# Attention and two dense layers on one core: rounded q and k made and moved two slots sooner, a bank of its own for head 0's unread products, residues of heads 1 and 2 on GpSimd

## The chip, the cores and the metric

The kernel runs on 1 core of a Trainium2 chip. The metric is the device time of one execution in microseconds (us). TensorE does the matmuls, VectorE (DVE in the rows), ScalarE (ACT) and GpSimd (POOL) the elementwise work, SyncE (SP) issues nearly all transfers. A matmul of TensorE writes to PSUM, in eight banks; the other data are in SBUF. Each engine takes its own instructions in the order in which they are written; between engines there are semaphores, placed by the framework where two instructions touch the same data.

## The reference

Attention for 2 batches, 8 heads, 768 positions and a head size of 64, with a mask by hash buckets; then two dense layers (512 to 2048 to 512) over 1536 tokens. Cut to what matters here:

```
q_bits = (einsum('bhsd,dk->bhsk', q, proj) > 0)      # 6 bits a position
k_bits = (einsum('bhsd,dk->bhsk', k, proj) > 0)
mask   = bucket(q_bits)[:, :, :, None] == bucket(k_bits)[:, :, None, :]
scores = where(mask, q @ k.T / sqrt(D), -1e9)
attn   = exp(scores - max(scores)); attn /= sum(attn) + 1e-9
x      = attn @ v                                    # then the dense layers
x      = (g(x @ w_in)) @ w_out                       # g = h * tanh(softplus(h))
x      = (P(x @ w_in2) / Q(x @ w_in2)) @ w_out2
```

## The kernel before, in words

**Numbers in two parts.** Matmuls run on float32 numbers that are rounded for TensorE (fp32r). A value is therefore kept as a rounded part ("hi") and a residue ("lo" = value - rounded part). For a head h, raws[h] holds k on partitions 0 to 63 and q on partitions 64 to 127. From it the kernel makes:

- qB[h % 4], by hi(h) on ScalarE (line 229, helper line 61): the rounded k and q. Later its rows 0 to 31 are overwritten with the signs of the codes, by code_q(h), two ScalarE activations (line 329).
- qX[h % 4], by lo(h) (line 234): the residue. The helper is lo_dve on VectorE (line 70) or lo_pool on GpSimd (line 67); the table ENG names VectorE for "lo".
- KK[h % 4], two planes of k: move_k(h) (line 241) is a DMA that copies the rounded k, qB rows 0 to 63, into rows 64 to 127 of both planes (384 KB in the DMA's count). For head 0 two ScalarE activations, khi, do that (line 237). move_x(h) (line 247) copies the residue of k into the second plane, move_h(h) (line 251) copies rounded q to the lower half of qX. code_k(h) (line 320, two VectorE instructions) writes the code rows of the first plane.

**The codes.** codes(h) (line 298) multiplies raws[h] with the projection into a PSUM tile "cp", of the tag "dn", which has one bank. code_k(h) reads the k half of it, code_q(h) the q half. For head 0 the product is made twice, and code_q reads the second copy, in the tile "wm" of the tag "pv" (one bank too). That tile is also the one that warm(n) writes: small matmuls whose results nobody reads (line 314), issued to keep TensorE at work in the start.

**The loop over keys.** For each head and each of 6 chunks of 128 keys: smax(h, c) (line 343) multiplies for the largest score, and VectorE reduces it (line 347); fin_a and fin_b (lines 353 to 365) turn the maxima into a row of qB[h % 4], by two DMAs on SP's queue and two on GpSimd's; st(h, c) (line 376) makes the scores, ScalarE the exponential (line 381); pv(h, c) (line 393, helper line 287) multiplies with v; dsum(h, c) (line 402) sums the exponentials into the tile "dn", of the same single bank as the codes. At the head's end evac and devac (lines 418 and 427) copy the results out of PSUM on ScalarE, gather(h) (line 436) brings the sums together by two small DMAs, recip(h) (lines 448 to 454) inverts them on VectorE.

**The order.** All of that is written out by hand in slots, six to a head. The table `order` (line 535) gives each step the slot, relative to the head's first st, in which its first piece is issued; within a slot the steps go in the order of the table's lines. Slots modulo 6 are called slot 0 to 5 here. In the steady state:

- slot 0: hi's new place; slot 1: fin_a, fin_b, evac, devac, move_h, and move_k's new place
- slot 2: hi's old place, codes, code_k, gather; slot 3: move_k's old place, lo
- slot 4: code_q, recip; slot 5: dsum (two pieces of the three), move_x, load

Heads 0 to 2 and head 1's first chunks are issued ahead of slot 0, in the order of the tuple `start` (line 599). There, an entry with a name in the set DVE_LO gets lo_dve as its helper, which the table ENG would give it as well.

Beside the heads, `weights` converts the first dense layer's weights (int64 words that hold float64 numbers), one part of a tile every six slots: load, three VectorE instructions (lines 100 to 106), two on GpSimd (lines 64 and 67), stores to a scratch for the first three tiles. The dense layers (lines 628 to 851) come after the heads.

Of the kernel before, what the change touches and what calls it, by code (L numbers as in the profile page):

```python
# [9 lines left out]
F32 = mybir.dt.float32  # L10
# [12 lines left out]
HALF = S // 2  # L23
# [4 lines left out]
NBITS = 6  # L28
EARLY, SHARED, FIRST = 7, 3, (78, 66, 72, 60, 60, 60, 60)
W_AT, W_LEAD = 7, 4  # L30
DVE_LO = (("lo", 0),)
ENG = dict(
    lo="dd", hi="aa", xhi="a", xlo="dd", whi="pppp", wlo="pppp",
)
# [10 lines left out]
def attention_moe_moe(ctx: ExitStack, tc: tile.TileContext, kq, v, proj2, cst, eye, w1, w2, ab, out):  # L45
    nc = tc.nc

    def pool(stack, name, bufs=1, **kw):
        return stack.enter_context(tc.tile_pool(name=name, bufs=bufs, **kw))
# [120 lines left out]
    def attention(actx, tctx):  # L170
# [10 lines left out]
        ps = pool(actx, "ps", 3, space=PSUM)  # L181
        pvp = pool(actx, "pv", 1, space=PSUM)
# [11 lines left out]
        ones = v_p.tile([128, 32], F32, tag="ones", name="ones")  # L194
        wones = v_p.tile([128, 128], F32, tag="wones", name="wones")

        def memsets():
            nc.vector.memset(ones, 1.0)
            nc.vector.memset(wones, 1.0)
            nc.gpsimd.memset(cs_t, 0.0)  # L200
            nc.gpsimd.memset(cs_t[:, 1:2], -1.0)
            nc.gpsimd.memset(cs_t[:, 2:3], 1.0)
            for i in range(4):
                nc.gpsimd.memset(f32(KK[i])[32:64, 0], 0.0)
            for i in range(2):
                nc.gpsimd.memset(f32(SM[i]), 0.0)
            nc.gpsimd.memset(bias[:, 1:2], 1.000001)
# [77 lines left out]
        def both(o, w, x, start=False, stop=False):  # L285
            for a in range(2):
                nc.tensor.matmul(out=o[64 * a:64 * a + 64, 0:HALF], lhsT=w, rhs=qhalf(x, a), start=start, stop=stop)  # L287
# [7 lines left out]
        ct = {}  # L295


        def codes(h):
            if not 0 <= h < B * H:
                return  # L300
            ct[h] = [pvp.tile([128, 512], F32, tag="dn", name="cp")] * 2
            if h == 0:
                ct[h][1] = warm_up[0]
            for t in ct[h][0:1 + (h == 0)]:
                both(t, p_raw, raws[h], start=True, stop=True)


        warm_up = []

        def warm(n):  # L310
            if not warm_up:
                warm_up.append(pvp.tile([128, 512], F32, tag="pv", name="wm"))
            for _ in range(n):
                nc.tensor.matmul(out=warm_up[0][0:32, HALF:512], lhsT=ones, rhs=wones, start=True, stop=True)  # L314

        def code_k(h):
            if not 0 <= h < B * H:
# [202 lines left out]
        def first(f, n):  # L520
# [16 lines left out]
            ("smax", smax, -11, 6),  # L537
            ("fin_a", fin_a, -5, 1),
            ("fin_b", fin_b, -5, 1),
            ("hi", hi, -16, 1),  # L540
            ("move_k", move_k, -15, 1),
            ("lo", lo, -15, 1),
            ("codes", codes, -16, 1),
            ("pv", pv, (3, 3, 5, 5, 7, 7), 6),
            ("dsum", dsum, (5, 5, 5, 5, 7, 7), 6),
# [41 lines left out]
        def slot_ops(g):  # L587
            for name, fn, k in slots.get(g, ()):
                if (name, k) not in done:
                    fn(*k)  # L590
# [5 lines left out]
        def coef():  # L596
            nc.scalar.activation(out=babs, in_=ab_t[:, 4:6], func=ACT.Abs)

        start = (
            ("load", 0), ("get", 0), ("get", 1), ("load", 1), ("load", 2), ("warm", 5), ("hi", 0), ("codes", 0),  # L600
            ("khi", 0, 0), ("lo", 0), ("warm", 5), ("code_k", 0), ("code_q", 0), ("hi", 1), ("khi", 0, 1), ("get", 2),
            ("move_k", 1), ("lo", 1), ("move_x", 0), ("smax", 0, 0), ("warm", 2), ("smax", 0, 1), ("warm", 2), ("hi", 2),
            ("smax", 0, 2), ("warm", 2), ("move_k", 2), ("lo", 2), ("move_h", 0), ("smax", 0, 3), ("warm", 2),
            ("smax", 0, 4), ("warm", 2), ("smax", 0, 5), ("codes", 1), ("fin_a", 0), ("fin_b", 0), ("code_q", 1),
            ("code_k", 1), ("load_v", 0), ("move_x", 1), ("load", 3), ("warm", 8), ("smax", 1, 0), ("smax", 1, 1),
            ("move_h", 1), ("coef",),
        )

        def run():
            memsets()  # L610
            fns = {o[0]: o[1] for o in order}
            fns.update(get=get, coef=coef, khi=khi)
            for name, *k in start:
                if name == "warm":
                    warm(*k)
                    continue
                done.add(("move_k" if name == "khi" else name, tuple(k[:1]) if name == "khi" else tuple(k)))
                fns[name](*k, **({"fn": lo_dve} if (name, *k) in DVE_LO else {}))
            for g in range(last):
                slot_ops(g)  # L620

        def tail(i):
            for g in {1: range(last, last + 3), 2: range(last + 3, last + 5), 4: range(last + 5, last + 30)}.get(i, ()):
                slot_ops(g)

        return run, tail

    def moe(mctx, tctx, tail):
# [224 lines left out]
    with tc.manual_schedule():  # L853
        nc.scalar.preload_act_table_set("natural_log_exp_and_others")
        tctx = ExitStack()
        with ExitStack() as actx:
            run, tail = attention(actx, tctx)
            run()
        with ExitStack() as mctx:
            run = moe(mctx, tctx, tail)  # L860
            run()
# [55 lines left out]
```

## Time and profile before

| what | value |
|---|---|
| median of 3 runs | 820.53 us |
| the three runs | 820.53, 812.40, 820.99 us |
| the profiled execution | 819.36 us, of which its span, first to last instruction, is 817.6 us |
| TensorE busy | 784.3 us (96%) |
| VectorE, ScalarE, GpSimd busy | 593.8, 424.9, 65.4 us |
| first st matmul of head 0 | at 21.95 us |
| first matmul of the dense layers | at 287.43 us |

Times in rows are us from the span's start unless marked ns. Groups of instructions are told by line of the kernel, engine, operation, and output<-input by the program's names. "[2.60 <-ACT qB L329]" behind a row says that the engine was idle for 2.60 us before it and that ScalarE's instruction of line 329 ended that idle time. Such releasers are inferred from semaphore events. A busy TensorE is not one at full speed: PEclk is the mean granted clock as a share of the full one, and of the two levels, 2.4 and 1.2 GHz, the lower reads 0.5. At the start of a span, before the first change of level, the record shows 1.00 whatever the level was.

### The profile page before, as it was taken

The numbers are of one execution on the slowest core, as the hardware profiler recorded it, in microseconds if no ns is written. First come the engines' busy times: TensorE is split into PE (matmuls) and PEld (weight loads), VectorE is DVE, ScalarE is ACT, GpSimd is POOL, SyncE is SP. The second block draws the span as 40 slices with busy tenths as digits, with TensorE's granted clock in tenths as the row PEclk, the third lists the DMA queues.
The fourth block names the chain that finished last, engine by engine and source line by source line (L and its number), as shares of the span: only waits on it lengthen the run. The fifth ranks groups of instructions, "written<-read, shape, count | busy, mean of one in ns | idle before, by whom it ended". The sixth has DMA issues, their size and how long they took to land.

```text
span 817.6 us, 10933 instructions
## 1 busy us (share of the span) xinstructions
PE 784.3 (96%) x3804; PEld 577.2 (71%) x3804; DVE 593.8 (73%) x1102; ACT 424.9 (52%) x684; POOL 65.4 (8%) x98
## 2 busy tenths in 40 slices
PE   8888989899989999999999999999999999999998
PEld 4444545455545577888888888887788888888886
DVE  5565677678775269965555667739999888888886
ACT  3344555456545544432122224448887766777674
POOL 2212132222221100000000000000000000000000
PEclk9899999999999999999999999999999999999999
DMA  4735455554564044442545467750000100001001
GB/s 117 201 103 156 130 139 149 152 143 121 146 176 138 22 127 128 144 141 81 176 156 153 149 202 248 233 162 26 0 1 1 52 1 1 1 1 52 1 0 52
DMA packets 57030, 85.49 MB, mean 105 GB/s; under 512 B 20496, under 2 KB 28688, under 8 KB 56976
## 3 DMA queue, kind: packets, MB, share of 16 engines
q1 hardware_dynamic: 55952, 84.77, 35.5%
q8 instruction: 30, 0.49, 0.3%
q14 instruction: 24, 0.20, 0.1%
q0 software_dynamic: 1024, 0.03, 0.1%
HBM read 57.71 MB, written 14.73 MB: 89 GB/s over the span
## 4 chain that ended last, share of the span: by engine, by line
PE 84%; DMA 6%; DVE 4%; ACT 3%; issue 1%; SPq 1%; POOL 0%; ACTq 0%; DVEq 0%
PE h L661 29%; PE y L681 16%; PE y L679 14%; PE sp L376 8%; DMA kk<-qB 6%; PE pv L287 5%; PE dn L402 5%; PE mp L343 4%; PE cp L287 2%; ACT qB L329 2%; PE wm L314 1%; DVE t L103 1%; DVE w L70 1%; DVE r L106 1%; DVE t L100 0%
## 5 line engine op out<-in xcount | busy, mean ns | idle before, releaser
L661 PE MATMUL h<-xh,w 128*128 128x512 f32 x768 | 205.0, 389 | 0.0
L661 PEld LDWEIGHTS h<-xh,w 128*128 128x128 f32 x768 | 144.1, 188 | 30.6 <-issue 0.6
L347 DVE TENSOR_REDUCE m<-mp 128x1 f32<-128x768 f32 x96 | 90.9, 954 | 73.3 <-PE mp L343 72.7
L381 ACT ACTIVATE e<-sp 128x768 f32<-128x768 f32 x96 | 77.2, 811 | 73.6 <-PE sp L376 73.2
L70 DVE TENSOR_TENSOR gl<-ep,gh 128x512 fp32r<-128x512 f32 x96 | 65.9, 686 | 61.5 <-ACT ep L705 60.8
L704 ACT ACTIVATE gh<-h 128x512 fp32r<-128x512 f32 x48 | 28.7, 598 | 154.6 <-PE h L661 141.5
L661 PE MATMUL h<-xl,w 128*128 128x512 f32 x384 | 102.7, 389 | 0.0
L681 PE MATMUL y<-w,gh 128*128 128x512 f32 x384 | 96.3, 389 | 0.0
L679 PE MATMUL y<-gh,w 128*128 128x512 f32 x384 | 94.8, 389 | 0.0
L661 PEld LDWEIGHTS h<-xl,w 128*128 128x128 f32 x384 | 72.1, 188 | 15.0
L679 PEld LDWEIGHTS y<-gh,w 128*128 128x128 f32 x384 | 72.1, 188 | 15.0
L681 PEld LDWEIGHTS y<-w,gh 128*128 128x128 f32 x384 | 72.1, 188 | 14.9
L287 PE MATMUL pv<-e,vf 128*64 128x384 f32 x384 | 72.5, 499 | 0.0
L402 PE MATMUL dn<-e,ones 128*32 128x384 f32 x384 | 42.2, 547 | 22.0 <-ACT qB L329 22.0
L376 PE MATMUL sp<-qB,kk 128*128 128x384 f32 x192 | 56.7, 376 | 1.6 <-DMA qB<-stt 1.1
L376 PEld LDWEIGHTS sp<-qB,kk 128*128 128x128 f32 x192 | 31.7, 194 | 37.2 <-issue 19.1
L711 ACT ACTIVATE ep<-h 128x512 f32<-128x512 f32 x48 | 28.5, 594 | 52.4 <-PE h L661 52.4
L106 DVE SCALAR_TENSOR_TENSOR r<-r,t 128x256 int32<-128x256 int32 (+1 forms) x114 | 52.2, 458 | 4.7
L343 PE MATMUL mp<-kk,qB 128*128 128x384 f32 x192 | 53.3, 360 | 2.1 <-issue 1.5
L103 DVE SCALAR_TENSOR_TENSOR t<-r,t 128x256 int32<-128x256 int32 (+1 forms) x114 | 52.2, 458 | 3.9
L681 PE MATMUL y<-w,gl 128*128 128x512 f32 x192 | 53.3, 392 | 0.5 <-DVE gl L70 0.4
L679 PE MATMUL y<-gl,w 128*128 128x512 f32 x192 | 51.6, 390 | 1.6 <-DVE gl L70 1.6
(78 smaller groups left out, 1010.2 us busy)
## 6 DMA issues: line engine op xcount, KB each, us to landing
r<-w SPq DMA_DIRECT2D x100, 256.0 KB
w<-r SPq DMA_DIRECT2D x64, 128.0 KB
w<-w SPq DMA_DIRECT2D x16, 512.0 KB
r<-w SPq DMA_DIRECT2D x14, 512.0 KB
kq<-kq SPq DMA_DIRECT2D x16, 384.0 KB
kk<-qB SPq DMA_DIRECT2D x15, 384.0 KB
kk<-qX SPq DMA_DIRECT2D x16, 192.0 KB
qX<-qB SPq DMA_DIRECT2D x16, 192.0 KB
```

The source lines that it names most:

```text
L70: nc.vector.tensor_tensor(out=o, in0=i, in1=f32(h), op=ALU.subtract)
L103: lambda: nc.vector.scalar_tensor_tensor(out=t, in0=r[:, :, 1], scalar=-0x40000000, in1=t, op0=ALU.bitwise_and, op1=ALU.bitwise_or),
L106: lambda: nc.vector.scalar_tensor_tensor(out=o, in0=r[:, :, 0], scalar=29, in1=t, op0=ALU.logical_shift_right, op1=ALU.bitwise_or),
L287: nc.tensor.matmul(out=o[64 * a:64 * a + 64, 0:HALF], lhsT=w, rhs=qhalf(x, a), start=start, stop=stop)
L343: nc.tensor.matmul(out=p[:, a, 0:HALF], lhsT=qB[h % 4][:, c * 128:(c + 1) * 128], rhs=qhalf(KK[h % 4][:, 0], a), start=True, stop=True,)
L347: nc.vector.tensor_reduce(out=mt[h][:, c:c + 1], in_=halves(p), op=ALU.max, axis=AX.XY)
L376: nc.tensor.matmul(out=p[:, a, 0:HALF], lhsT=kk[:, c * 128:(c + 1) * 128], rhs=qq[:, a * HALF:(a + 1) * HALF], start=(i == 0), stop=(i == 1),)
L381: nc.scalar.activation(out=wide(e), in_=halves(p), func=ACT.Exp, scale=1.0 / D ** 0.5)
L402: nc.tensor.matmul(out=pvt[h, "d"][32 * n:32 * n + 32, 0:HALF], lhsT=ones, rhs=qhalf(pt[h, c - 1 + n // 2], n % 2), start=(c == 1), stop=( ...
L661: nc.tensor.matmul(out=p, lhsT=w[:, c * 128:(c + 1) * 128], rhs=x[:, c, :], start=(n == 0), stop=(n == 11))
L679: nc.tensor.matmul(out=y[m], lhsT=w[:, DM + m * 128:DM + (m + 1) * 128], rhs=g, **s)
L681: nc.tensor.matmul(out=y[m], lhsT=g[:, m * 128:(m + 1) * 128], rhs=w[:, DM:2 * DM], **s)
```

## The change

- In the steady order, hi moves from slot -16 to -18 and move_k from -15 to -17, both relative to the head's first st. This holds for heads 3 to 15.
- In the start, lo of heads 1 and 2 gets lo_pool, GpSimd's helper; DVE_LO goes.
- warm writes to a tile of the pool "s" until the codes of head 0 are issued; the second copy of head 0's product has a tile "wm" of its own in "pv", which warm uses from then on.
- The start is written in another order: code_q(0) ahead of code_k(0) and of warming, which is cut there from 5 pairs to 1; hi(1), lo(1), hi(2), lo(2) sooner; move_x(0), move_h(0), move_k(1), load(3) in that order on SP; move_k(2) behind fin_b(0); code_q(1) ahead of smax(0, 5).

```diff
-DVE_LO = (("lo", 0),)
+POOL_LO = (("lo", 1), ("lo", 2))
...
             ct[h] = [pvp.tile([128, 512], F32, tag="dn", name="cp")] * 2
             if h == 0:
-                ct[h][1] = warm_up[0]
+                ct[h][1] = pvp.tile([128, 512], F32, tag="pv", name="wm")
...
         def warm(n):
-            if not warm_up:
-                warm_up.append(pvp.tile([128, 512], F32, tag="pv", name="wm"))
+            if 0 in ct:
+                t = ct[0][1]
+            else:
+                if not warm_up:
+                    warm_up.append(ps.tile([128, 2, 512], F32, tag="s", name="wm"))
+                t = warm_up[0][:, 0]
             for _ in range(n):
-                nc.tensor.matmul(out=warm_up[0][0:32, HALF:512], lhsT=ones, rhs=wones, start=True, stop=True)
+                nc.tensor.matmul(out=t[0:32, HALF:512], lhsT=ones, rhs=wones, start=True, stop=True)
...
-            ("hi", hi, -16, 1),
-            ("move_k", move_k, -15, 1),
+            ("hi", hi, -18, 1),
+            ("move_k", move_k, -17, 1),
...
-            ("khi", 0, 0), ("lo", 0), ("warm", 5), ("code_k", 0), ("code_q", 0), ("hi", 1), ("khi", 0, 1), ("get", 2),
-            ("move_k", 1), ("lo", 1), ("move_x", 0), ("smax", 0, 0), ("warm", 2), ("smax", 0, 1), ("warm", 2), ("hi", 2),
-            ("smax", 0, 2), ("warm", 2), ("move_k", 2), ("lo", 2), ("move_h", 0), ("smax", 0, 3), ("warm", 2),
-            ("smax", 0, 4), ("warm", 2), ("smax", 0, 5), ("codes", 1), ("fin_a", 0), ("fin_b", 0), ("code_q", 1),
-            ("code_k", 1), ("load_v", 0), ("move_x", 1), ("load", 3), ("warm", 8), ("smax", 1, 0), ("smax", 1, 1),
-            ("move_h", 1), ("coef",),
+            ("khi", 0, 0), ("lo", 0), ("code_q", 0), ("code_k", 0), ("warm", 1), ("hi", 1), ("lo", 1), ("khi", 0, 1),
+            ("get", 2), ("move_x", 0), ("smax", 0, 0), ("warm", 2), ("move_h", 0), ("hi", 2), ("lo", 2), ("smax", 0, 1),
+            ("move_k", 1), ("warm", 2), ("smax", 0, 2), ("load", 3), ("warm", 2), ("smax", 0, 3), ("codes", 1),
+            ("smax", 0, 4), ("warm", 2), ("code_q", 1), ("smax", 0, 5), ("fin_a", 0), ("fin_b", 0), ("code_k", 1),
+            ("warm", 6), ("move_k", 2), ("load_v", 0), ("move_x", 1), ("smax", 1, 0), ("smax", 1, 1), ("move_h", 1),
+            ("coef",),
...
-                fns[name](*k, **({"fn": lo_dve} if (name, *k) in DVE_LO else {}))
+                fns[name](*k, **({"fn": lo_pool} if (name, *k) in POOL_LO else {}))
```

## Rows read from the trace of the kernel before

**Rows 1.** The page: TensorE's total; the chain that ended last, by line.

```profile
PE 784.3 (96%) x3804; PEld 577.2 (71%) x3804; DVE 593.8 (73%) x1102; ACT 424.9 (52%) x684; POOL 65.4 (8%) x98
...
PE h L661 29%; PE y L681 16%; PE y L679 14%; PE sp L376 8%; DMA kk<-qB 6%; PE pv L287 5%; PE dn L402 5%; PE mp L343 4%; PE cp L287 2%; ACT qB L329 2%; PE wm L314 1%; DVE t L103 1%; DVE w L70 1%; DVE r L106 1%; DVE t L100 0%
```

**Rows 2.** TensorE's waits: waiter, waited for, us in total, times, longest.

```profile
PE dn L402 <- ACT qB L329: 22.0, 11, 4.0
...
PE mp L343 <- DVE m L347: 0.4, 1, 0.4
```

**Rows 3.** ScalarE's waits, the same columns.

```profile
ACT qB L329 <- DMA kk<-qB: 29.6, 9, 4.9
...
ACT qB L329 <- DVE rc L452: 2.9, 2, 1.5
```

**Rows 4.** Timeline of one head: start, us, engine, line, op [idle before <-releaser].

```profile
102.77 1.56 SPq L362 DMA_DIRECT2D qB<-stt  x2
102.88 1.17 ACT L418 ACTIVATE ev<-pv,vsc 64x384 f32<-64x384 f32 x2 [1.10 <-PE pv L287]
...
105.06 1.15 SPq L436 DMA_DIRECT2D cs<-dv  x2
...
105.39 0.85 ACT L61 ACTIVATE qB<-kq 128x768 fp32r<-128x768 f32 x1
...
108.47 0.66 SPq L241 DMA_DIRECT2D kk<-qB  x1
...
111.01 0.21 DVE L448 TENSOR_TENSOR rc<-cs 24x32 f32<-24x32 f32 x1
...
114.14 1.16 ACT L329 ACTIVATE qB<-cp,cst 32x384 fp32r<-32x384 f32 x2 [3.50 <-DMA kk<-qB]
...
115.35 1.50 PE L402 MATMUL dn<-e,ones 128*32 128x384 f32 x16 [2.60 <-ACT qB L329]
```

**Rows 5.** Windows, dn to dn: length, busy (records) by engine, PEclk, DMA, GB/s.

```profile
38.99:60.54 21.55, 17.58 (x95) 10.18 (x95) 13.20 (x22) 8.49 (x13) 2.99 (x4) 0.91 0.41 113
60.54:80.89 20.35, 16.69 (x92) 8.98 (x93) 11.27 (x20) 8.51 (x13) 5.16 (x7) 0.92 0.60 158
80.89:97.47 16.58, 16.30 (x88) 8.58 (x88) 10.71 (x20) 8.51 (x13) 2.99 (x4) 0.91 0.42 123
...
149.23:165.39 16.16, 16.16 (x88) 8.54 (x88) 10.36 (x19) 9.27 (x13) 3.01 (x4) 0.91 0.37 103
...
181.30:196.06 14.76, 14.76 (x88) 8.22 (x88) 11.70 (x22) 9.29 (x13) 3.00 (x4) 1.00 0.48 131
```

**Rows 6.** Timeline of the head with the longest transfer of move_k.

```profile
67.23 1.52 SPq L362 DMA_DIRECT2D qB<-stt  x2
...
72.90 0.66 SPq L241 DMA_DIRECT2D kk<-qB  x1
...
79.68 1.16 ACT L329 ACTIVATE qB<-cp,cst 32x384 fp32r<-32x384 f32 x2 [4.57 <-DMA kk<-qB]
```

**Rows 7.** Timeline of the start.

```profile
6.83 2.27 PE L314 MATMUL wm<-wones,ones 128*32 128x128 f32 x10
9.18 1.18 ACT L329 ACTIVATE qB<-wm,cst 32x384 fp32r<-32x384 f32 x2 [3.68 <-PE wm L314]
...
11.12 0.96 DVE L70 TENSOR_TENSOR qX<-kq,qB 128x768 fp32r<-128x768 f32 x1 [4.02 <-ACT qB L61]
...
12.11 2.69 DVE L347 TENSOR_REDUCE m<-mp 128x1 f32<-128x768 f32 x3
...
16.72 1.93 PE L314 MATMUL wm<-wones,ones 128*32 128x128 f32 x16
...
18.84 1.55 SPq L362 DMA_DIRECT2D qB<-stt  x2
...
21.95 0.59 PE L376 MATMUL sp<-qB,kk 128*128 128x384 f32 x2 [1.07 <-DMA qB<-stt]
```

**Rows 8.** Groups by line: GpSimd's subtraction of 128x512; columns busy us, mean ns.

```profile
L67 POOL TENSOR_TENSOR w<-r,w 128x512 fp32r<-128x512 f32 x8 | 10.3, 1288 | 0.7
```

## The prediction

> **What bounds the kernel now.** I read the totals and the chain that ended last first. TensorE is busy for 784 of 817.6 us, and the chain is TensorE's, with one stranger in it: a transfer, `kk<-qB`, which holds 6% of the span [rows 1]. So TensorE is the bound, and what can be won is time in which it waits or runs slowly. The waits of TensorE come next: one line of them is large, 22.0 us in 11 pieces, `dn` (line 402) waiting for ScalarE's `qB` (line 329); the nearest wait on VectorE's reduction is 0.4 us [rows 2]. Then I asked what that ScalarE instruction waits for: nine times the landing of `kk<-qB`, 29.6 us, and twice it is put down to a VectorE instruction, 2.9 us [rows 3]. Line 329 is code_q, line 241 is move_k. code_q overwrites rows 0 to 31 of qB, which the transfer of move_k reads, so it may not start before that transfer has landed; ScalarE takes its work in order; and dsum needs the "dn" bank, whose codes code_q has still to read. That is the whole loop.
>
> The reader sees it in one head [rows 4]: hi on ScalarE at 105.39 (slot 2), the transfer issued at 108.47 (slot 3), code_q (slot 4) idle for 3.50 and started at 114.14, `dn` idle for 2.60 and started at 115.35. ScalarE waits 3.50 and TensorE 2.60, so the first 0.90 of such a wait costs nothing.
>
> The last view is the one by heads, cut from one `dn` of slot 5 to the next [rows 5]. A head without a stall takes 14.76 us, all of it TensorE's. Heads with a stall take more, and four stretches also show a mean granted clock of 0.91 or 0.92: during the stall TensorE falls to the lower of its two levels, and works there for some microseconds after. So a stall costs twice.
>
> **The change, part by part.**
>
> *hi and move_k two slots sooner (heads 3 to 15).* No instruction is added: 13 activations and 13 transfers change places. What they gain is read from SP's queue. move_k's new slot, 1, is also fin_b's, and fin_b comes first, so the earliest that move_k can be issued is the end of fin_b's two DMAs on SP: 102.77 + 1.56 = 104.33 instead of 108.47, 4.1 us sooner against a stall of 2.60 [rows 4]. The tightest head is the one with the longest transfer: issued at 72.90, code_q started at 79.68, so landed after some 6.7 us, in company with a load of v and weight stores. There fin_b ends at 67.23 + 1.52 = 68.75; 68.75 + 6.7 = 75.5, while ScalarE was free for code_q at 79.68 - 4.57 = 75.1 [rows 6]. That leaves a wait of 0.4, within the free 0.90. In its new place the transfer is ahead of that company, so 6.7 is the pessimistic duration. I take the stall as gone in all 11 heads.
>
> Term one: **-22.0 us** [rows 2]. Term two, the clock: a stretch of length L at mean clock c loses about (1 - c) x L, so 0.09 x 21.55 + 0.08 x 20.35 + 0.09 x 16.58 + 0.09 x 16.16 = 1.9 + 1.6 + 1.5 + 1.5 = **-6.5 us**. The check: the last two do the same 88 matmul records as the head without a stall, in 16.30 and 16.16 against 14.76, 1.5 and 1.4 more [rows 5].
>
> What covers the moved instruction itself: hi (0.85) now stands in slot 0 between two exponentials; behind it are the next exponential and evac, and ScalarE sat idle for 1.10 before evac, waiting for TensorE [rows 4]. It fits there; with that cover gone the price would be up to 0.85 in 13 heads, 11 us. hi needs qB of four heads before, whose last reader is the matmul of the slot before; the exponential ahead of hi in ScalarE's queue waits for a later matmul, so no wait is added.
>
> What move_k is now ahead of, on SP: move_h and gather. Both are issued some 0.7 us later and their data follow a 384 KB transfer. move_h is needed five slots later. Gather was issued at 105.06 and the first instruction on its result, `rc<-cs`, ran on VectorE at 111.01 [rows 4], 5.9 us later; that is a margin and not a measured wait. What is late after the stall has gone: VectorE, busy 11.70 of 14.76 us in the head without a stall [rows 5], has 3.06 us to give before it becomes the limit. I cost this part at nothing, and the other end is the rival below.
>
> *The start.* Before, code_q of head 0 waited for ten warming instructions that write the bank it reads: they started at 6.83 and code_q at 9.18, after 3.68 idle, though its products were ready at about 6.9 [rows 7]. Now code_q is issued ahead of warm and reads at about 6.95; its two activations (1.18) end at 8.1 instead of 10.36. Then one warm pair and the two matmuls, and the first reduction at about 9.3. Before, that reduction started at 12.11, because the residue of head 1 (0.96 from 11.12) stood ahead of it on VectorE, and that of head 2 cost another 0.96 later. GpSimd now makes both: a GpSimd subtraction of 512 columns takes 1.29 us [rows 8], so 768 columns about 1.9 each, 9.0 to 13 in all, beside the reductions. With VectorE freed, three reductions in 2.69 make 0.90 each, and TensorE sets the pace: matmuls, warming pairs and gaps, about 1.1 us per chunk as before (an estimate from the start's timeline), and head 1's products once, 0.9. Five chunks and the products end at 9.3 + 5.8 = 15.1, the last reduction at 16.0, fin_b on SP at 16.6 instead of 18.84: 2.2 us sooner.
>
> Against it stands the clock. Ten warming instructions took 2.27 us at 6.83 but sixteen took 1.93 at 16.72 [rows 7]: 0.23 each against 0.12, so TensorE was still on its lower level at 6.83. With nine of those ten gone it idles for about 1.2 us instead, and may rise later: two chunks at the lower level cost 0.7 each, 1.4; all five and the products, 4.4. So the start's bounds are -2.2 (risen at once) and +2.2 (never risen); I take two slow chunks, **-0.8**.
>
> move_k of head 2 and the load of v go out after fin_b, and code_q of head 1 has from about 10 to 15 for its transfer; I put nothing on them.
>
> Sum: -22.0 - 6.5 - 0.8 = -29.3. The profiled execution took 819.36 us (span 817.6): 819.4 - 29.3 = 790.1. It is 1.2 under the median of the runs, so the forecast for the median is **791**. The dense layers start sooner by the same amount and are the same work, bound by TensorE.
>
> **Rivals.**
>
> *The start eats some.* The clock stays low, or GpSimd's 1.9 us residues, its share of fin_b's DMAs behind them, make head 1 late. For it: the warming ahead of the first products is cut from ten instructions to two. Against: the start can only lose its own few microseconds; 819.4 - 28.5 + 2.2 = 793, with a late transfer for the first heads up to 797.
>
> *Part of the stall stays.* move_k still stands behind fin_b, which itself waits for VectorE; with no stalls VectorE has less time to catch up, fin_b comes later, and code_q finds the transfer in flight again. If each of 11 heads keeps 1.0 us, and half of the clock loss stays: -11 - 3.3 - 0.8 gives 804. Against it: the head without a stall issued its work on time at 11.70 busy.
>
> *Slower: the gather.* The transfer of 384 KB and move_h's 192 KB are now ahead of gather. If gather's data wait for them, it lands at 104.33 + 6.7 + some 2 = 113 instead of before 111.01; VectorE, in order, stands still for 2 us in slot 4 with reductions behind it, TensorE waits for those, and its clock falls (1.5 as above). From the point where VectorE's lag exceeds its 3.06 us it goes to TensorE in full: (2 + 1.5) x 12 heads = 42, less 29.3, that is +13: 832. Against it: VectorE's reserve covers 2 us in each head. The Trainium skill, "DMA: Bandwidth & Descriptors", section "Queues, rings and completion order", says that each DMA engine takes descriptors of a queue in ring order; by that rule the gather does wait behind the moved transfer, which speaks for this rival. No run here shows yet by how much.
>
> *Nothing happens.* The inferred cause is wrong and code_q waits for something else, as in the two cases put down to VectorE [rows 3]: 819 to 820. Against it: nine of eleven name the transfer.
>
> **How the numbers follow.** Forecast 0.72 (786 to 795), start 0.12, part of the stall 0.10, gather 0.03, nothing 0.03. A measurement of this kernel tells about 1% (8 us) from no change; all but the last two cases are faster by more than that: faster 0.94, same 0.03, slower 0.03. The range: the low end is both terms and the best start, 819.4 - 28.5 - 2.2 = 789, less 5, because one of the three runs before lay 8 us under the others: 784. The high end takes in most of the rival in which part of the stall stays: 803.
>
> **What would show it.** Right: `dn` waiting for `qB` gone or under 2 us; code_q no longer idle on `kk<-qB`; heads of 14.8 to 15.3 us each, none with a mean clock under 0.95 after the first; the first `sp` at about 20 instead of 21.95. Wrong: `rc<-cs` idle on `cs<-dv` in every head (the gather), `dn` still idle on `qB` by a microsecond per head, or a first reduction that starts no sooner than 12.

## The result and the profile after

| | before | changed |
|---|---|---|
| median of 4 runs | 819.25 us (812.40 to 820.99) | **791.88 us** (791.12 to 794.09) |
| profiled execution (span) | 819.36 us (817.6) | 791.69 us (789.8) |
| first `sp` of head 0 | 21.95 us | 19.67 us |

The ratio is 0.9685, 95% interval [0.9625, 0.9746]. In a later session the same changed kernel took 792.16 us (791.46 to 798.86, 6 runs), ratio 0.9705 [0.9668, 0.9742]. The forecast was 791.

The page of the changed kernel: engine totals, then the chain that ended last, by line.

```profile
PE 774.2 (98%) x3788; PEld 572.4 (72%) x3788; DVE 593.7 (75%) x1100; ACT 422.5 (53%) x684; POOL 71.6 (9%) x100
...
PE h L665 29%; PE y L685 16%; PE y L683 15%; PE sp L380 9%; PE pv L287 8%; PE mp L347 5%; PE dn L406 4%; PE cp L287 2%; DVE w L70 1%; DVE m L351 1%; DMA kk<-qB 1%; DVE t L103 1%; DMA vf<-v 1%; DVE r L106 1%; DVE gl L70 1%
```

Against [rows 1] the stranger in the chain, `kk<-qB`, has gone from 6% to 1%. TensorE is busy for 10 us less, with only 16 records fewer: part of what was won is work done at a higher clock. Lines behind the diff are numbered four higher now: dsum is line 406, code_q 333, smax 347.

Waits of the changed kernel: waiter, waited for, us in total, times, longest. The first two are TensorE's, the third ScalarE's.

```profile
PE mp L347 <- DVE m L351: 2.3, 6, 0.5
PE dn L406 <- ACT qB L333: 1.8, 1, 1.8
...
ACT qB L333 <- DMA kk<-qB: 3.4, 1, 3.4
```

The 11 waits of [rows 2] have become one, and the nine of [rows 3] one. In their place stand six small waits of smax on VectorE, where there was one.

**Where the 27.8 us of span came from.** Both spans are cut at the same events: the first `sp`, the first `dn` of slot 5, and the `dn` behind the last code_q, which is three heads before the dense layers. Before, from the first `sp` on:

```profile
21.95:38.99 17.04, 14.13 (x65) 8.54 (x65) 10.06 (x15) 7.01 (x11) 5.43 (x8) 0.90 0.82 210
38.99:246.46 207.47, 187.50 (x1087) 104.53 (x1087) 144.28 (x252) 106.48 (x155) 49.34 (x66) 0.97 0.54 143
```

The changed kernel, with the start as well (length, then TensorE's busy time with its records first):

```profile
0.00:19.67 19.67, 14.53 (x68) 7.91 (x69) 11.23 (x17) 7.79 (x11) 8.24 (x18) 1.00 0.43 124
19.67:35.15 15.48, 12.63 (x65) 7.81 (x65) 9.99 (x15) 7.00 (x11) 3.23 (x5) 1.00 0.80 208
35.15:218.69 183.54, 181.81 (x1090) 102.81 (x1094) 143.31 (x250) 104.82 (x155) 52.94 (x68) 1.00 0.59 160
```

- The start: 21.95 - 19.67 = 2.28.
- The first head up to its `dn`: 17.04 - 15.48 = 1.56, of which 14.13 - 12.63 = 1.50 is the same 65 matmul records at a clock of 1.00 instead of 0.90. TensorE's idle time there hardly changed (2.91 and 2.85): this head kept its stall.
- The stretches of the next twelve heads: 207.47 - 183.54 = 23.93. Idle time fell from 19.97 to 1.73, by 18.24. Busy time fell from 187.50 to 181.81, by 5.69, for as many records (1087 and 1090): that is the clock.
- What follows, the last three heads and the dense layers: 571.14 and 571.11 us, 0.03. It was only moved.

2.28 + 1.56 + 23.93 + 0.03 = 27.80, the whole.

One head of the changed kernel shows the mechanism that [rows 4] showed with the stall. Timeline: start, us, engine, line, operation.

```profile
99.92 0.84 ACT L61 ACTIVATE qB<-kq 128x768 fp32r<-128x768 f32 x1
...
102.07 1.54 SPq L366 DMA_DIRECT2D qB<-stt  x2
...
103.79 0.69 SPq L241 DMA_DIRECT2D kk<-qB  x1
...
105.17 1.87 SPq L440 DMA_DIRECT2D cs<-dv  x2
...
109.50 1.16 ACT L333 ACTIVATE qB<-cp,cst 32x384 fp32r<-32x384 f32 x2
...
109.83 0.17 DVE L452 TENSOR_TENSOR rc<-cs 24x32 f32<-24x32 f32 x1
...
111.52 0.85 PE L406 MATMUL dn<-e,ones 128*32 128x384 f32 x8
```

hi now stands ahead of fin_b, move_k right behind it, and code_q and `dn` have no bracket any more: neither waited. code_q starts 5.71 us after move_k's issue. gather is issued at 105.17, behind move_k, and `rc<-cs` has no bracket either. A row at the end of a view counts only what lies inside the view: this `dn` has 16 matmuls too.

Windows from `dn` to `dn` of the changed kernel, against [rows 5]:

```profile
66.35:81.12 14.77, 14.77 (x92) 8.24 (x96) 10.72 (x20) 8.29 (x12) 4.51 (x7) 1.00 0.71 197
81.12:96.83 15.71, 15.36 (x96) 8.72 (x100) 11.66 (x22) 9.22 (x14) 4.04 (x5) 1.00 0.57 155
```

No such stretch has a clock below 1.00 any more. The head of 15.71 has one of the new waits of smax, 0.35 (its row is below), and four matmul records more than the one of 14.77.

**The stall that stayed** is in the first head. Timeline of the changed kernel:

```profile
25.51 2.63 SPq L216 DMA_DIRECT2D kq<-kq  x2
28.23 0.62 SPq L241 DMA_DIRECT2D kk<-qB  x1
...
33.93 1.16 ACT L333 ACTIVATE qB<-cp,cst 32x384 fp32r<-32x384 f32 x2 [3.37 <-DMA kk<-qB]
35.15 1.18 PE L406 MATMUL dn<-e,ones 128*32 128x384 f32 x12 [1.76 <-ACT qB L333]
```

This is move_k of head 3. SP had first to issue the loads of heads 4 and 5, which together take 2.63 us on SP, so the transfer left at 28.23 and code_q waited for it. The forecast measured the new slot by fin_b alone, which in the steady state is the last thing ahead of move_k; in the first head it is not.

**The longest stall went by another path** than the forecast's. In the first two heads the table gives fin_b slot 3 and not slot 1, so the new place of move_k is ahead of fin_b there. SP in the second head, whose stall is the 4.0 of [rows 2]; two rows before the change, then two after it:

```profile
53.82 1.50 SPq L362 DMA_DIRECT2D qB<-stt  x2
55.50 0.69 SPq L241 DMA_DIRECT2D kk<-qB  x1
...
39.16 0.66 SPq L241 DMA_DIRECT2D kk<-qB  x1
...
48.41 1.48 SPq L366 DMA_DIRECT2D qB<-stt  x2
```

Before, move_k went out right behind fin_b. By the forecast's measure, the end of fin_b (55.32), it could have gone only 0.2 us sooner, and the stall would have stayed. In fact it now goes out 9.25 us ahead of fin_b.

**The start.** Timeline of the changed kernel:

```profile
7.08 1.16 ACT L333 ACTIVATE qB<-wm,cst 32x384 fp32r<-32x384 f32 x2 [1.49 <-PE wm L287]
...
9.18 0.62 PE L318 MATMUL wm<-wones,ones 128*32 128x128 f32 x4
9.29 4.27 DVE L351 TENSOR_REDUCE m<-mp 128x1 f32<-128x768 f32 x4 [2.11 <-PE mp L347]
...
16.59 1.56 SPq L366 DMA_DIRECT2D qB<-stt  x2
...
19.67 0.59 PE L380 MATMUL sp<-qB,kk 128*128 128x384 f32 x2 [1.05 <-DMA qB<-stt]
```

code_q starts at 7.08 instead of 9.18 [rows 7], the first reduction at 9.29 instead of 12.11, fin_b at 16.59 instead of 18.84. GpSimd's residues take 1.80 us each.

### The profile page after: what moved, and what is told of

It reads as the page before. It is cut to its first block, busy times and chain, and to the rows that moved or that the text cites. A ratio compares the mean times of both kernels' runs of the same rounds, so it can differ in the third digit from the quotient of the medians.

```text
span 789.8 us, 10934 instructions
## 1 busy us (share of the span) xinstructions
PE 774.2 (98%) x3788; PEld 572.4 (72%) x3788; DVE 593.7 (75%) x1100; ACT 422.5 (53%) x684; POOL 71.6 (9%) x100
## 4 chain that ended last, share of the span: by engine, by line
PE 88%; DVE 6%; DMA 2%; ACT 1%; issue 1%; SPq 1%; POOL 0%; DVEq 0%; ACTq 0%
PE h L665 29%; PE y L685 16%; PE y L683 15%; PE sp L380 9%; PE pv L287 8%; PE mp L347 5%; PE dn L406 4%; PE cp L287 2%; DVE w L70 1%; DVE m L351 1%; DMA kk<-qB 1%; DVE t L103 1%; DMA vf<-v 1%; DVE r L106 1%; DVE gl L70 1%
## 5 line engine op out<-in xcount | busy, mean ns | idle before, releaser
L717 DVE TENSOR_TENSOR n<-n,ep 128x512 f32<-128x512 f32 x48 | 33.1, 690 | 26.9 <-ACT n L716 26.9
```

What stands on the lines that cost most here:

```text
L717: nc.vector.tensor_tensor(out=v_, in0=v_, in1=u, op=ALU.mult)
```

## The experiments

The theory: all of the gain beyond the start is move_k's place on SP; the clock's part is a consequence of the stall; the start is worth what TensorE's level in it allows. Rivals: the start is what matters; it is hi's place; the gather pays.

**1. The moves alone.** The kernel before with the two new slots and the old start.

```diff
-            ("hi", hi, -16, 1),
-            ("move_k", move_k, -15, 1),
+            ("hi", hi, -18, 1),
+            ("move_k", move_k, -17, 1),
```

> The kernel before with hi and move_k two slots sooner and nothing else of the change. Theory (the loss was the loop move_k, code_q, dn bank; the start is a second, separate gain): dn's wait for qB falls from 22.0 us in 11 waits to about 2 in one (the first head, whose move_k stays behind loads on SP), mean clock back to 1.00 from the second head on; about 24 us less than before, 795. Rival (the moved transfer gains only together with the new start, which brings VectorE and SP ahead): waits of 0.5 to 2 us stay in most heads, 805 to 812.

Measured: 793.88 us (792.90 to 795.02), ratio 0.9692 [0.9665, 0.9719], and no wait of `dn`. The moves alone bring all of the gain that the times can show: the interval takes in both ratios of the changed kernel, 0.9685 and 0.9705. The first head keeps a wait here too, in another place:

```profile
30.37 0.87 PE L287 MATMUL cp<-kq,pr 128*64 128x384 f32 x4 [1.82 <-ACT qB L329]
```

With the old start the load of head 3 comes late: hi of head 3 waits 4.30 us for it, code_q of head 2 stands behind hi on ScalarE, and the products of head 3 need the bank that code_q still reads.

**2. The start alone.** The changed kernel with the two old slots (-16 and -15).

> The changed kernel with hi and move_k back at their old slots: the new start alone. Theory: the first sp at 19.7 as in the changed kernel, dn's waits as before (about 22 us in 11), 2 to 4 us less than before: 816. Rival (the new start is what freed the heads): the waits fall, under 808.

Measured: 818.30 us (810.77 to 822.99, 10 runs), ratio 0.9995 [0.9961, 1.0030]. Alone, the new start is worth nothing that can be measured; the expected 2 to 4 us did not come. The waits of `dn` are there as before, 20.8 us in ten. In the profiled execution the first head's stall takes back what the start gave:

```profile
33.92 0.69 SPq L241 DMA_DIRECT2D kk<-qB  x1
...
38.94 1.36 PE L406 MATMUL dn<-e,ones 128*32 128x384 f32 x12 [3.79 <-ACT qB L333]
```

The `dn` starts at 38.94, as before at 38.99 [rows 5], though the first `sp` was 0.5 us sooner (21.44, and not the 19.7 expected, because TensorE worked on its lower level until 12.6); its wait of 3.79 is set by a transfer issued at 33.92.

**3. hi alone.** The kernel before with hi at -18 and move_k left at -15.

> The kernel before with hi two slots sooner and move_k where it was. Theory (the transfer's issue counts, and it was not held by hi but by its own slot on SP): dn still waits 18 to 22 us, 816 to 820. Rival (ScalarE's order is the point: hi in slot 2 held up what follows): most of the wait goes, 800 or less.

Measured: 818.72 us (815.55 to 821.10, 10 runs), ratio 0.9992 [0.9971, 1.0014]. Its largest wait of TensorE:

```profile
PE dn L402 <- ACT qB L329: 22.4, 11, 3.9
```

The eleven waits are all there. The rounding was never late; what was late is the slot in which SP issues the transfer.

**4. One slot instead of two.** The kernel before with hi at -17 and move_k at -16.

> The kernel before with hi and move_k one slot sooner each. By SP's queue move_k then stands behind move_h of slot 1 and ahead of gather, some 0.6 us later than two slots sooner and still 2 to 3.5 us sooner than before. Theory (a stall goes as soon as the shift exceeds wait less 0.9): most waits go, a rest of 0 to 4 us beside the first head's, 795 to 799. Rival (each slot is worth half): about 807.

Measured: 793.66 us (790.31 to 794.38), ratio 0.9681 [0.9649, 0.9712], and no wait of `dn`. Timeline of a head:

```profile
88.68 1.52 SPq L362 DMA_DIRECT2D qB<-stt  x2
...
91.00 0.67 SPq L241 DMA_DIRECT2D kk<-qB  x1
...
96.58 1.16 ACT L329 ACTIVATE qB<-cp,cst 32x384 fp32r<-32x384 f32 x2
```

One slot does as much as two. move_k is issued 2.32 us behind fin_b here, where [rows 4] have 5.70: 3.38 sooner. With the 0.90 that cost nothing this covers a stall of 4.28, and the longest of [rows 2] was 4.0. The gain is a threshold, not so much per slot; the expectation had left 0 to 4 us of stalls for this case, and none is left.

**5. The clock's part by itself.** The kernel before, with the stalls left in and matmuls on constants issued while TensorE would idle, in the heads in whose wake the clock fell. They add no result: they go into a part of a tile that nobody reads.

```diff
             if c == 1:
+                for _ in range({0: 7, 1: 14, 2: 14, 6: 10}.get(h, 0)):
+                    nc.tensor.matmul(
+                        out=pvt[h][0:32, HALF:512], lhsT=ones, rhs=wones, start=False, stop=True,
+                        skip_group_check=True,
+                    )
```

> The kernel before, with small matmuls issued ahead of dsum in the four heads after whose stall the mean granted clock was 0.91 or 0.92 (7, 14, 14 and 10 of them, two instructions of about 0.12 us each, so 1.7, 3.4, 3.4 and 2.4 us of work that fits into the stall). Theory (a stall costs twice, and the second price is the clock, 6.5 us): dn starts when it did, the stretches after read 0.99 or 1.00, and the time falls by 4 to 6.5 us, to 812 to 814. Rival (the clock is only a companion, what is slow there is VectorE or the buffers): no gain, 818 or a little more.

Measured: 812.64 us (810.92 to 814.88, 10 runs) beside 816.53 for the kernel before in that session, ratio 0.9937 [0.9912, 0.9962]. Windows of this kernel, from `dn` to `dn`:

```profile
38.55:58.53 19.98, 19.17 (x122) 12.18 (x123) 13.21 (x22) 8.51 (x13) 3.00 (x4) 1.00 0.44 120
58.53:77.10 18.57, 18.47 (x121) 11.70 (x121) 11.34 (x20) 8.52 (x13) 5.17 (x7) 1.00 0.64 170
77.10:92.65 15.55, 14.81 (x89) 8.22 (x89) 11.16 (x20) 8.52 (x13) 3.00 (x4) 1.00 0.45 135
...
110.05:126.53 16.48, 16.37 (x89) 8.70 (x89) 10.53 (x19) 8.50 (x13) 3.00 (x4) 0.90 0.48 138
...
144.17:158.92 14.75, 14.75 (x88) 8.24 (x88) 10.35 (x19) 9.30 (x13) 3.00 (x4) 1.00 0.41 118
```

The four stretches that read 0.91 or 0.92 in [rows 5] read 1.00 and are shorter by 1.57, 1.78, 1.03 and 1.41: 5.8 us, where the forecast had 6.5. In the profiled execution the clock fell in two other stretches, from 110.05 (0.90) and from 239.61 (0.89), so that less is left of it in the total. The stalls themselves were left in: ScalarE still waits 26.9 us in nine pieces for `kk<-qB`, against 29.6 [rows 3]. A stall in this kernel does cost twice, and the second part is repaired without touching the first.

**6. The residues back on VectorE.** The changed kernel with `POOL_LO = ()`.

> The changed kernel with the residues of heads 1 and 2 on VectorE again. Theory (they stood ahead of reductions): fin_b of head 0 and the first sp come 1 to 2 us later, 793 to 794. Rival (the reductions are paced by TensorE and there is room for the residues): the first sp within 0.3 us of 19.67, no difference, 792.

Measured: 795.24 us (792.70 to 797.43), ratio 0.9731 [0.9695, 0.9768]. That looks like a price of 3 us, but the profile shows another cause: until 18 us every smax pair took 1.01 us instead of 0.62, and VectorE's reductions waited for TensorE. Experiment 9 shows the same with the residues on GpSimd. Who makes the residues stays undecided.

**7. Warming ahead of code_q.** The changed kernel with ten warming matmuls between lo(0) and code_q(0). They write the tile that code_q reads, as before the change.

```diff
-            ("khi", 0, 0), ("lo", 0), ("code_q", 0), ("code_k", 0), ("warm", 1), ("hi", 1), ("lo", 1), ("khi", 0, 1),
+            ("khi", 0, 0), ("lo", 0), ("warm", 5), ("code_q", 0), ("code_k", 0), ("warm", 1), ("hi", 1), ("lo", 1), ("khi", 0, 1),
```

> The changed kernel with five warming pairs again between the products of head 0 and code_q, into the same bank. Theory (code_q waited for the warming): code_q of head 0 starts at about 9.3 instead of 7.08 and the first sp comes about 2 us later, 794. Rival (the warming is worth its time, the clock rises sooner): no later than 19.7, 792.

Measured: 794.76 us (794.64 to 794.89), ratio 0.9727 [0.9700, 0.9753]: 2.9 us more than the changed kernel's first median. The intervals overlap, so the time alone does not show a price; the timeline does:

```profile
9.04 1.16 ACT L333 ACTIVATE qB<-wm,cst 32x384 fp32r<-32x384 f32 x2 [3.48 <-PE wm L318]
```

code_q waits for the warming again, 3.48 us as against 3.68 [rows 7], and fin_b comes at 18.54 instead of 16.59. So the place of code_q ahead of the warming is worth about 2 us in the start. The four runs lie within 0.25 us.

**8. More in front of the gather.** The changed kernel with one more transfer of 384 KB issued on SP just ahead of gather's two; nobody reads it.

```diff
+            x = scratch.tile([64, 2, S], F32, tag="extra", name="extra")
+            if h + 3 < B * H:
+                nc.sync.dma_start(out=x, in_=f32(KK[(h + 2) % 4])[64:128])
```

> The changed kernel with one more transfer of 384 KB (k of a later head to a scratch) on SP ahead of gather in each head. Theory (gather has a margin, the moved transfer used little of it): rc<-cs waits for cs<-dv by 0 to 2 us a head and TensorE by nearly nothing, 792 to 796. Rival of the prediction (gather behind large transfers stops VectorE, and TensorE with it): rc waits 2 to 5 us in every head, TensorE 1 to 3, 810 to 830.

Measured: 798.41 us (797.30 to 799.52), ratio 0.9776 [0.9743, 0.9808], 6.3 to 6.5 us over the changed kernel's two medians and above the 796 that was expected at most. Timeline:

```profile
108.29 1.19 SPq L440 DMA_DIRECT2D extra<-kk  x1
109.53 2.52 SPq L443 DMA_DIRECT2D cs<-dv  x2
...
111.00 0.62 PE L380 MATMUL sp<-qB,kk 128*128 128x384 f32 x2 [0.61 <-ACT e L385]
...
113.40 0.18 DVE L455 TENSOR_TENSOR rc<-cs 24x32 f32<-24x32 f32 x1 [2.00 <-DMA cs<-dv]
```

VectorE now does stand still at `rc<-cs`, 2.00 us in this head and less in the others but the last. The only wait of TensorE that follows it in that stretch is the 0.35 of a smax, which the changed kernel has too. The time is lost elsewhere. Waits of this kernel, one of TensorE's and one of VectorE's:

```profile
PE sp L380 <- ACT e L385: 5.6, 10, 0.6
...
DVE rc L455 <- DMA cs<-dv: 19.2, 12, 8.4
```

Of the 19.2 us, 8.4 are the last head's, where TensorE does not wait for it (in the changed kernel this one wait is 9.2); the other eleven are about 1 us each on average (0.20 to 2.00). TensorE pays 5.6 us in ten waits on the exponential, the `sp` at 111.00 among them; one of the ten, 0.5, is in the changed kernel as well. So the gather does come late behind a transfer ahead of it, but up to 2.0 us of that is within VectorE's reserve: the rival was right that it comes late, and wrong on the price. Why it comes late is not settled: SP ended the issue of the gather 1.9 us later than without the added transfer (1.24 until it starts, and 2.52 instead of 1.87 for itself), which is about as long as `rc` waited. The nine new waits are of the kind that comes next.

**What the six waits are.** smax, st and their readers take turns in three PSUM buffers of the tag "s". Five of the six waits, 0.35 each, are new; the sixth, 0.5, is in the first head, where the kernel before has one of 0.35. The five stand at the first smax of a slot 1, in every second head. The instruction lists of the two built programs show what it waits for in such a head, and the banks of the four tiles up to it. In the program before, this smax waits for a transfer and the exponential; in the changed one, for a transfer and VectorE:

```
before: L343 MATMUL mp_866<-kk2_129,qB2_121 128x384 [waits DMAHW5_49,Activation_49]
after:  L347 MATMUL mp_860<-kk2_129,qB2_121 128x384 [waits DMAHW0_49,DVE_49]
banks before: sp_845:4 mp_852:0 sp_858:2 mp_866:4
banks after:  sp_838:4 mp_845:0 sp_852:2 mp_860:0
```

The framework did not keep the rotation: it gave smax bank 0, which VectorE's reduction of the slot before frees, in place of bank 4, which the exponential frees. In the changed kernel's timeline that reads:

```profile
84.85 0.62 PE L347 MATMUL mp<-kk,qB 128*128 128x384 f32 x2 [0.35 <-DVE m L351]
```

Experiments 1 and 4 have six such waits too (2.1 us each), and their lists the same change in every second head, so the waits come with the moves and not with the start. The list of experiment 8 settles its nine new waits as well: each of them is at an `sp` that was given the bank of the `sp` just before it, which the last exponential had still to read.

**9. The changed kernel again.**

> The changed kernel as it is, beside the next three on the same chip. Theory (in the start TensorE may or may not rise to its higher level after the idle 1.3 us ahead of the first smax, from execution to execution): the first sp at 19.7 when it has risen, about 24 when not; times between 790 and 796. Rival (the start is the same in all executions): within 1 us of each other, 791 to 792.

Measured: 792.16 us; the six runs were 798.86, 792.08, 792.11, 791.46, 794.19 and 792.21. The profiled one is the first, 5 to 7 us over the others. Timeline:

```profile
8.30 0.64 PE L318 MATMUL wm<-wones,ones 128*32 128x128 f32 x2 [1.30 <-ACT qB L333]
8.87 1.01 PE L347 MATMUL mp<-kk,qB 128*128 128x384 f32 x2
9.80 1.06 PE L318 MATMUL wm<-wones,ones 128*32 128x128 f32 x4
...
24.00 0.59 PE L380 MATMUL sp<-qB,kk 128*128 128x384 f32 x2 [1.06 <-DMA qB<-stt]
```

Up to 8.30 its instructions start when those of the first profile do. There the four warming matmuls at 9.18 took 0.62; here those at 9.80 take 1.06, and the smax pair goes from 1.01 to 0.62 only at 18.71. TensorE stayed at its lower level for ten microseconds longer, with the same code, and the first `sp` comes at 24.00 instead of 19.67: 4.3 us of the 7. Another 1.5 is the stall of the first head, 3.26 instead of 1.76.

**10. No gap in the start.** The changed kernel with six warming matmuls, in place of the two behind code_k, into the "s" bank, which nothing reads: they fill the 1.30 us in which TensorE waited for code_q.

```diff
+        def fill(n):
+            for _ in range(n):
+                nc.tensor.matmul(out=warm_up[0][0:32, 0, HALF:512], lhsT=ones, rhs=wones, start=True, stop=True)
...
-            ("khi", 0, 0), ("lo", 0), ("code_q", 0), ("code_k", 0), ("warm", 1), ("hi", 1), ("lo", 1), ("khi", 0, 1),
+            ("khi", 0, 0), ("lo", 0), ("code_q", 0), ("code_k", 0), ("fill", 3), ("hi", 1), ("lo", 1), ("khi", 0, 1),
```

> The changed kernel with three warming pairs in place of one, in the bank that nobody reads, so that TensorE works through the 1.3 us in which it stood idle for code_q of head 0. Theory (the clock's rise is a matter of that gap): smax starts no later than 8.8, always on the higher level or soon after, times within 1 us of each other, 790 to 792. Rival (the rise is chance with or without the gap): the same spread as the changed kernel.

Measured: 790.56 us (789.68 to 792.28), ratio 0.9674 [0.9644, 0.9704]; the six runs lie within 2.6 us. Timeline, and the window of the first head:

```profile
6.94 1.49 PE L312 MATMUL wm<-wones,ones 128*32 128x128 f32 x6
...
9.12 0.62 PE L322 MATMUL wm<-wones,ones 128*32 128x128 f32 x4
...
19.63:35.68 16.05, 15.37 (x64) 9.84 (x64) 10.07 (x15) 7.40 (x11) 3.25 (x5) 0.80 0.90 218
```

TensorE works through from 6.94 and is on the upper level by 9.12, and code_q is not made later. But then it fell: the first head has a mean clock of 0.80, and takes 16.05 us without any wait of `dn`, where the first profile of the changed kernel has 15.48 with one. The intervals of 9 and 10 overlap. The spreads do not tell them apart either: the 7.4 us of experiment 9 are one run of six, without it the spread is 2.7.

**11. Head 3 sooner.** The changed kernel with hi(3) behind code_q(1), and move_k(3) on SP behind move_x(1), in the start: ahead of the loads that held it back.

> The changed kernel with hi and move_k of head 3 issued in the start, ahead of move_h of head 1 and the loads of heads 4 and 5 that held move_k of head 3 on SP until 28.23. Theory (the one stall that is left is that queue): dn's wait for qB, 1.8 us, is gone, 790. Rival (the transfer meets the load of v and move_x there and the wait moves to another): no gain, 791.5 or more.

Measured: 793.57 us (790.45 to 795.26), ratio 0.9696 [0.9660, 0.9733]. The wait of `dn` is gone, but the time does not show it: the profiled start was on the lower level until 14.6, with its first `sp` at 22.60, and the first head then had a mean clock of 0.80 and took 16.05 us.

**12. Both, and one step of the plan.** 10 and 11 together, and `norm` a slot sooner (22 instead of 23), so that the framework chooses its banks anew.

> The changed kernel with the three warming pairs, head 3 sooner, and norm one slot sooner (slot 4), with which the framework gives the first smax of a head a buffer that ScalarE frees and not VectorE. Theory: dn's wait gone (1.8) and the six waits of smax on VectorE's reduction too (2.1), 788. Rival (norm in slot 4 stands ahead of the reductions, since VectorE then has recip and norm in one slot): waits of TensorE on VectorE of 2 us or more, 790 to 793.

Measured: **787.55 us** (786.17 to 789.11), ratio 0.9634 [0.9603, 0.9665], below the changed kernel's [0.9668, 0.9742] of the same session. It is the best of all. What is left of TensorE's waits on VectorE's reduction:

```profile
PE mp L351 <- DVE m L355: 0.5, 1, 0.5
```

No wait of `dn` is left, and of the six smax waits only the one of the first head; in the list of this program the first smax of slot 1 waits for the exponential in every head. Which of the three edits gives how much of the 3.0 us against experiment 10 was not measured one by one.

## Why the prediction was right, step by step

**What bounds the kernel** was read rightly. Moving the transfer's issue alone (1, 4) takes the stalls away, moving the rounding alone (3) does not.

**Term one, -22.0.** "I take the stall as gone in all 11 heads" held for ten. The eleventh is head 0's, where two loads stand ahead of move_k on SP; 1.8 of its 2.0 us stayed, so the term came out at -20.2. The step that failed is the one that took fin_b's end as the earliest moment of issue in every head: in the first two heads fin_b does not stand ahead of move_k's new place. In one of them the stall stayed. In the other, the longest of all, the same measure gave 0.2 us against a stall of 4.0; that this one went was luck for the sum, and the head of [rows 6] was not the tightest. It was not free either: 1.9 us came back as new waits of smax on VectorE (0.4 before, 2.3 after), which the forecast priced at nothing. It had looked at what is queued behind the moved instructions on SP and ScalarE, and not at how the banks would be given out.

**Term two, the clock, -6.5.** It measured 5.7 in the twelve stretches behind the first head by busy time, and 5.8 in experiment 5 without the stalls being touched. The rule (1 - c) x L is a little high for a stretch with a stall in it, because L counts idle time, in which no work is slowed: 0.09 x 17.58 + 0.08 x 16.69 + 0.09 x 16.30 + 0.09 x 16.16 gives 5.8 by the busy times of [rows 5]. Left out was the head before the first `dn`, 1.50. That this belongs to the change is not shown: the first head's mean clock was 0.89 to 0.91 in the five profiles with the old start, but with the new one 1.00 in four and 0.80 to 0.89 in five (experiments 7, 8, 10, 11 and 12).

**Term three, the start, -0.8,** was sized for two slow chunks; the profiled start had none, and 2.28 came. The pieces were right: first reduction at "about 9.3" (9.29), fin_b at "16.6" (16.59), GpSimd's residues "about 1.9 each" (1.80). The warming that goes is eight instructions of the ten, not nine. What the text could not know is TensorE's level: the bounds of -2.2 and +2.2 were its two outcomes, and both happened, -2.28 in the first profile and 24.00 - 21.95 = +2.05 in experiment 9, with the same program. In the medians the start does not show: experiment 1, with the old one, has the changed kernel's ratio.

By terms: 20.2 - 1.9 of waits, 5.7 + 1.5 of clock and 2.3 of start make 27.8, as the windows of the two profiled executions say; the forecast was 29.3.

**The rivals.** "The start eats some" is what single executions do, not the median. "Part of the stall stays" holds for one head. "Nothing happens" fell. "Slower: the gather" fell in the changed kernel, where `rc<-cs` waits only in the last head, and experiment 8 tells by how much: a further 384 KB makes VectorE wait about 1 us for it and 2.00 at the most, under the 3.06 us that the prediction named as the point of decision. The Trainium skill, "DMA: Bandwidth & Descriptors", section "Queues, rings and completion order", says that a DMA engine takes the descriptors of a ring in its order. Experiment 8 fits that but does not show it, since SP's own issue came late by as much.

## What to carry to other kernels

Where an engine overwrites what a transfer still reads, the chain of waits names the compute instruction, but the remedy is the transfer's place in its issue queue: look at what is ahead of it there in every head, the first ones too. Price a stall with the clock that falls behind it, by busy time and not by length. And after any change of a plan look for new short waits on pooled PSUM buffers, since the order in which they are given out can change with it.

## What was not expected

- TensorE's level in the start is not decided by the program alone: with instructions at the same times up to 8.30 us it was on the upper level by 9.18 in one execution and not before 18 in another, 4.3 us apart at the first `sp`. What decides it stays open: with the gap of 1.30 us worked through, the level rose early in the profiled execution and fell again behind the first `sp`. The windows of the start read 1.00 in both executions of the changed kernel; only the durations (0.62 or 1.01 for an smax pair) tell them apart.
- A transfer that nobody waits for cost some 6.4 us (experiment 8). Most of it, 5.1 us in the profile, is in nine new waits of at most 0.6 us on a PSUM buffer, which come from the choice of buffers, as the five of the changed kernel do.
